# Where a slot's second score matmul stands, and how the prologue and the mixer's channels are arranged

## The chip, the cores and the metric

The kernel runs on one core of a Trainium2 chip. The metric is the device time in microseconds (us) of one execution. The five engines are TensorE (PE in the profile; PEld is its weight loading), VectorE (DVE), ScalarE (ACT), GpSimd (POOL) and SyncE (SP), which here only issues transfers. Each engine works through its own list of instructions in order, and semaphores tie the lists together. Before the change, three runs took 1406.85 to 1408.10 us, with a median of 1407.93 us.

## What is computed

This is one transformer block with adaptive layer norm, for 2048 tokens of width D = 640. Its attention has 32 heads of width 128 over a cache of 2048 keys and values; its MLP block is a token-shifting mixer (w1, w2) followed by an MLP (w3, w4) of width 1728.

```python
mod = (silu(c) @ w_mod).reshape(1, 6, 1, 640)      # six modulation vectors
sa, ca, ga, sb, cb, gb = ...                        # p = 0 .. 5
h = layernorm(x) * (1 + ca) + sa
q = h @ wq                                          # 32 heads x 128
p = softmax(q @ k_cache.T * 128 ** -0.5)            # per head, 2048 x 2048
x = x + ga * ((p @ v_cache) @ wo)
h = layernorm(x) * (1 + cb) + sb
u = gelu(layernorm(h) @ w1)                         # mixer: four groups of 160 channels,
                                                    # shifted by +1, -1, +2, -2 tokens
x1 = h + shifted(u) @ w2
x = x + gb * (x1 + gelu(layernorm(x1) @ w3) @ w4)
```

## The kernel before

The program is a list of operations. Each has an engine, what it reads and writes, and a key (the last number in the PE calls below). TensorE executes its operations in the order of their keys; the other engines' orders are found by a list scheduler inside the kernel, which also puts in the semaphore waits.

Attention is cut into 128 *steps*: 8 groups of 4 heads, 4 chunks of 512 tokens, 4 heads. A step has 8 *slots* (NP = 8). In a slot TensorE computes the scores of two key tiles of 128 keys against 512 queries (two matmuls of 512 columns into the two banks of one score tile), ScalarE takes the exp of the whole score tile, and TensorE multiplies earlier exps with the values (129 columns: 128 values and a column of ones for the row sum). There are two score tiles, S0 and S1, used in turn, so the scores of slot n+2 can be written once the exp of slot n is done.

```python
for j in range(NP):
    n = s * NP + j
    sp = Tile(pool="S%d" % (n % 2))
    pt = PT[n % NPT]
    for r in range(2):
        kt = 2 * j + r
        P.op("PE", <score matmul, 128x512>, ..., (K[b][kt // 4], q), (sp,), n + 0.01 * r, accum=True)
    x = P.op("ACT", <exp of sp into pt, 128x1024>, 1021, (sp,), (pt,), n)
    for r in range(2):
        u = 2 * j + r
        # slot: the slot in which key tile u is multiplied, PV_SLOTS = [2, 2, 3, 2, 2, 3, 2] tiles
        # in the slots 3 .. 9 after the step's start (8 and 9 are slots 0 and 1 of the next step)
        key = NP * s + 3 + slot + 0.3 + 0.01 * (u - acc)
        for bk in range(2):
            kb = key + 0.004 * bk if u < NKT - 2 else NP * s + 9.35 + 0.02 * bk + 0.001 * u
            P.op("PE", <two value matmuls, 128x129>, ..., (pt, V[b]), (o[bk],), kb, accum=True)
```

The query projection of the next step (five matmuls of 512 columns) has the keys `NP * s + 2.3 + 0.01 * kk`, so it stands in slot 2. The output projection of a chunk (32 matmuls of 320 columns) is spread over four later steps, with fractions of 0.6.

The prologue computes the first two modulation vectors as columns, from five pieces `wm[k]` of w_mod, normalises chunk 0 of x, transposes it on TensorE and makes the first query. `spin(n, key)` is n matmuls of ones that keep TensorE busy; their result is not used. Two of the other modulation vectors (p = 2 and 4) are loaded by ScalarE's queue into the buffers of heads 4 and 3 and are computed in the prologue and in step 0; p = 3 and 5 follow in steps 2 to 5.

```python
x0 = load_x2(0, -301, eng="ACT") + load_x2(2, -301)
...
P.op("POOL", <copy s_bc, broadcast>, 1000, (c_f,), (s_bc,), -290, lat=300)
spin(50, -298)
for k in range(KT):
    P.op("PE", mcol, ..., (wm[k], s_bf, ones), (mc,) + ..., -290 + k, accum=True)
# in ln1, chunk 0: transposes of x-hat, tiles 0 and 1 ahead of the last modulation piece
P.op("PE", tr, 330, ..., (-286.6 if i < 2 else -280) + 0.1 * i, accum=True)
# in ln1, the other chunks: statistics on VectorE, then rstd on ScalarE, then the DMA transpose to hT
rstd_act(g, a, a + 2, prio - 100, 0.0 if ch == 0 else 1500.0)
...
load_wq(0, 0, 1, -297)
load_k(0, -296, gate=(wm[2],))          # all pieces but the first wait for wm[2]
for p, b, pools, keys in ((2, NKV - 1, ("O0", "O1"), (-262, 0.5)), (4, NKV - 2, ("M", "M"), (1.5, 2.2))):
    ap = KV_t[:, b * KVW:b * KVW + KT * D].rearrange("p (k n) -> p k n", k=KT)
    dma("ACT", <w_mod vector p into ap>, 800, (wm[1],), tuple(K[b]) + (V[b],), -292 if p == 2 else -291)
    ...                                 # 2 x 5 matmuls of 320 columns per vector
    if p == 4:
        load_v(0, -290, "ACT", gate=(wm[1],))
load_wq(0, 1, HG, -295.985, gate=(wm[2],))
for n, p in enumerate((3, 5)):
    dma("SP", <w_mod vector p>, 800, ..., 8 + 12 * n, from_slot(8 + 12 * n))
    ...                                 # keys NP * (2 + 2 * n + hf) + 3.65 + k
```

After attention, TAIL gives the order of the parts: A is a w1 part of a chunk (25 matmuls of 512 columns), B a w2 tile of 128 tokens (10 of 320), WO the last output projection (32 of 320), I the layer norms of the last chunk, C a w3 part (70 of 512), D a w4 tile (28 of 320).

```python
TAIL = ("A0 B0 B1 B2 A1 B3 WO B4 B5 A2 B6 I3 B7 B8 C0 B9 D0 D1 D2 D3 C1 D4 A3 B10 B11 "
        "B12 B13 B14 D5 D6 D7 B15 C2 D8 D9 D10 D11 C3 D12 D13 D14 D15").split()
def w1_part(ch, key):                   # channels regrouped: 4 x 128 and the 4 x 32 that are left over
    for n in (4, 0, 1, 2, 3):
        ...                             # 5 matmuls into a bank of pool T (4 banks)
        if n == 4:
            P.op("ACT", <GELU of the left-over channels into rest>, ...)
            for g in range(4):
                P.op("DVE", <copy 32 rows of rest to us, shifted by DEL[g]>, 330, ...)
        else:
            P.op("ACT", <GELU of 128 channels of group n into us, shifted by DEL[n]>, ...)
```

Of the kernel before, what the change touches and what calls it, by code (L numbers as in the profile page):

```python
# [40 lines left out]
class Plan:  # L41
# [4 lines left out]
    HINT = {"PE": 300, "ACT": 40, "DVE": 60, "POOL": 1, "SP": 12}  # L46
# [116 lines left out]
    def emit(self, nc, es, ndma, redo, flag):  # L163
# [68 lines left out]
        def body(e):  # L232
            def f(eng):
                for i, o in enumerate(self.seq[e]):
                    if i == max(0, len(self.seq[e]) - self.HINT[e]):
                        hint[e] = eng.mark_branch_hint_location()
                    for sem, v in waits[o].items():
                        eng.wait_ge(sem, v)
                    ins = o.fn(eng)
                    if o.dma:  # L240
                        ins.then_inc(o.sem, 16)
                    elif o.needed:
                        ins.then_inc(o.sem, 1)
# [16 lines left out]
def fast_path(nc, es, flag, A_x, A_k_cache, A_v_cache, A_wq, A_wo, B_w1, B_w2, B_w3, B_w4, c, w_mod, out):  # L260
# [72 lines left out]
    us = [[T() for _ in range(KT)] for _ in range(NC)]  # L333
# [17 lines left out]
    w2b = tuple(T() for _ in range(4))  # L351
# [24 lines left out]
    def dma(eng, fn, kb, reads, writes, prio, need=(), after=()):  # L376
        return P.op(eng, fn, {"SP": 480, "ACT": 480, "POOL": 1000}[eng], reads, writes, prio, dma=True, kb=kb, need=need, after=after)
# [9 lines left out]
    def v_ones(i):  # L387
        P.op("POOL", lambda e: e.memset(V_ap[i][:, :, 128:130], 1.0), 200, (), (V[i],), -297 + i)
    for i in range(NKV - 2):
        v_ones(i)  # L390
# [16 lines left out]
    x0 = load_x2(0, -301, eng="ACT") + load_x2(2, -301)  # L407
# [29 lines left out]
    P.op("POOL", lambda e: e.tensor_copy(s_bc.ap, c_f.ap.unsqueeze(2).to_broadcast([128, KT, 128])), 1000, (c_f,), (s_bc,), -290, lat=300)  # L437
    spin(50, -298)
    for k in range(KT):
# [7 lines left out]
        P.op("PE", mcol, 2 * KT * (85 if k < KT - 1 else 62), (wm[k], s_bf, ones), (mc,) + ((warm,) if k < KT - 1 else ()), -290 + k, accum=True)  # L447
# [83 lines left out]
    def ln1(ch, prio):  # L531
        g = ln_slot()
        xs = x0 if ch == 0 else load_x2(4 * ch, XP[ch], from_slot(XS[ch])) + load_x2(4 * ch + 2, XP[ch], from_slot(XS[ch]))
        for a in (0, 2):
            for i in (a, a + 1):
                ln_stats(xs[i].ap, (xs[i],), g, i, prio, 0.0 if ch == 0 else 2000.0)
            rstd_act(g, a, a + 2, prio - 100, 0.0 if ch == 0 else 1500.0)
# [3 lines left out]
        if ch == 0:  # L541
# [5 lines left out]
            for i in range(4):  # L547
# [4 lines left out]
                P.op("PE", tr, 330, (xn[i], ident), (hp[0], hp[1], hq, hp[4]), (-286.6 if i < 2 else -280) + 0.1 * i, accum=True)  # L552
# [18 lines left out]
    def load_k(h, prio, gate=(), need=()):  # L571
        b = h % NKV
        for i in range(4):
            dmaT(lambda e, i=i: e.dma_start_transpose(K_ap[b][:, i * 512:(i + 1) * 512].unsqueeze(1), A_k_cache[0, h, i * 512:(i + 1) * 512, :]),
                 128, gate if i or h else (), (K[b][i],), prio + 0.01 * i, need)
# [5 lines left out]
    def load_wq(g, a, b, prio, need=(), gate=()):  # L581
        dma("SP", lambda e: e.dma_start(wq_t[g % 2][:, :, a * 128:b * 128],
                                        A_wq[:, (g * HG + a) * 128:(g * HG + b) * 128].rearrange("(k p) d -> p k d", p=128)),
            160 * (b - a), gate, tuple(wq[g % 2][a:b]), prio, need)
# [8 lines left out]
    load_k(0, -296, gate=(wm[2],))  # L593
    ln1(0, -280)


    def modulation(p, hf, w_ap, w_t, pool, key, prio):
        m = Tile(pool=pool)
        sl = slice(hf * HD, (hf + 1) * HD)
        for k in range(KT):  # L600
            P.op("PE", lambda e, k=k: e.matmul(m[:, 0:HD], s_bc[:, k, :], w_ap[:, k, sl], start=(k == 0), stop=(k == KT - 1)),
                 MM(HD), (s_bc,) + w_t, (m,), key(k), accum=True)
        P.op("DVE", lambda e: e.tensor_scalar_add(out=mod[p][hf].ap, in0=m[:, 0:HD], scalar1=1.0 if p == 4 else 0.0),
             490, (m,), (mod[p][hf],), prio)

    mod_src = lambda p: w_mod[:, p * D:(p + 1) * D].rearrange("(k p) n -> p k n", p=128)
    for p, b, pools, keys in ((2, NKV - 1, ("O0", "O1"), (-262, 0.5)), (4, NKV - 2, ("M", "M"), (1.5, 2.2))):
        ap = KV_t[:, b * KVW:b * KVW + KT * D].rearrange("p (k n) -> p k n", k=KT)
        held = tuple(K[b]) + (V[b],)
        dma("ACT", lambda e, ap=ap, p=p: e.dma_start(ap, mod_src(p)), 800, (wm[1],), held, -292 if p == 2 else -291)  # L610
        for hf in range(2):
            modulation(p, hf, ap, held, pools[hf], lambda k, a=keys[hf]: a + 0.01 * k, -50)
        v_ones(b)
        if p == 4:
            load_v(0, -290, "ACT", gate=(wm[1],))

    def load_head(h):
# [3 lines left out]
        load_k(h, pr, (wm[2],) if h == 1 else (), from_slot(n))  # L621
        load_v(h, pr + 1, gate=(wm[2],) if h == 1 else (), need=from_slot(n + 1))
# [6 lines left out]
    load_wq(0, 1, HG, -295.985, gate=(wm[2],))  # L629
# [5 lines left out]
    for n, p in enumerate((3, 5)):  # L635
        dma("SP", lambda e, n=n, p=p: e.dma_start(w_half[n], mod_src(p)), 800, (), (W12[n],) + w2b + tuple(wm), 8 + 12 * n, from_slot(8 + 12 * n))
        for hf in range(2):
            modulation(p, hf, w_half[n], (W12[n],) + w2b, "M", lambda k, n=n, hf=hf: NP * (2 + 2 * n + hf) + 3.65 + k, NP - 60)

    TAIL = ("A0 B0 B1 B2 A1 B3 WO B4 B5 A2 B6 I3 B7 B8 C0 B9 D0 D1 D2 D3 C1 D4 A3 B10 B11 "  # L640
            "B12 B13 B14 D5 D6 D7 B15 C2 D8 D9 D10 D11 C3 D12 D13 D14 D15").split()
    WOKEY = 3000 + 50 * TAIL.index("WO")
    WOD, CH, I3D = -200, -200, 0


    evac, last_ot = [], []
# [13 lines left out]
    def wo_group(g, ch):  # L660
# [3 lines left out]
        for qt in range(4):  # L664
            last_ot[:] = last_ot[-3:] + [dmaT(lambda e, qt=qt: e.dma_start_transpose(OT_ap[gs][:, qt], On_ap[gs][:, qt].rearrange("p h d -> p (h d)")),
                 128, (On[gs][qt // 2],), (OT[gs][qt],), s * NP - 100)]
# [37 lines left out]
    def step(s):  # L704
# [5 lines left out]
        if s == 0:  # L710
            q_proj(0, [-270 + kk for kk in range(KT)])
        if s + 1 < NS:
# [982 lines left out]
```

## Time and profile before

| | |
|---|---|
| median of 3 runs | 1407.93 us |
| span of the profiled execution | 1403.4 us |
| TensorE's mean granted clock | 0.993 |
| first exp starts | 15.88 us |
| step 8's first exp starts | 98.36 us |
| last value matmuls start | 1210.88 us |
| first w3 matmul starts | 1255.55 us |
| exps | 1024, mean 1023 ns |
| score matmuls | 2048, mean 379 ns |
| value matmuls | 8192, mean 220 ns |

How to read it. Times in the trace count from the span's start. A matmul's mean duration is longer than the distance from one to the next, because matmuls overlap in the array; so durations of matmuls must not be summed, and the distances between their starts say how fast they go. In a timeline a line gives the start, the time to the end of the group, the engine, the line of the program, the operation with output and inputs, the shapes, and the count; a bracket at the end is the idle time of the engine ahead of the group and what ended it. SPq and ACTq are transfers being issued by the engine's sequencer.

### The profile page before, as it was taken

To read this page: it belongs to the slowest core of one execution; us is meant where nothing else is said; L and a number is where in the kernel's file an instruction comes from. 1 tells how busy PE (TensorE), PEld (TensorE's weight loads), DVE (VectorE), ACT (ScalarE), POOL (GpSimd) and SP (SyncE) were. 2 spreads that over 40 slices of the span, in tenths; PEclk is the share of its full clock that TensorE was granted. 3 is DMA by queue.
4 is the path that set the end of the run, shared out by engine and by line. 5 is a ranking of instruction groups with operands and counts; after the bars stand their busy time and mean duration, and the time that the engine had idled before them with its cause. 6 is when DMAs were issued, how large, how long until landed. Compare 5 with 4: busy or idle time off the path is not lost.

```text
span 1403.4 us, 29645 instructions
## 1 busy us (share of the span) xinstructions
PE 1371.6 (98%) x12901; PEld 939.5 (67%) x13128; DVE 524.9 (37%) x1354; ACT 1106.3 (79%) x1179; POOL 125.3 (9%) x108
## 2 busy tenths in 40 slices
PE   8899999999999999999999999999999999999998
PEld 6566776667766676666766677666776676545554
DVE  4353323332233323333233332333223344577552
ACT  5788888888888888888888888888888888744222
POOL 0000000000000000000000000001233376600000
PEclk9999999999999999999999999999999999999999
DMA  9880512251213321241205121512253022411110
GB/s 242 173 154 16 99 35 46 35 102 39 46 35 79 62 46 35 50 91 30 51 17 102 31 41 33 106 35 46 54 106 98 16 35 52 109 33 38 39 47 25
DMA packets 259172, 88.83 MB, mean 63 GB/s; under 512 B 236705, under 2 KB 257762, under 8 KB 259042
## 3 DMA queue, kind: packets, MB, share of 16 engines
q1 hardware_dynamic: 255106, 83.77, 29.2%
q10 hardware_dynamic: 3936, 3.15, 0.8%
q8 instruction: 104, 1.70, 0.5%
q14 instruction: 26, 0.21, 0.1%
HBM read 43.48 MB, written 2.62 MB: 33 GB/s over the span
## 4 chain that ended last, share of the span: by engine, by line
PE 95%; DMA 2%; ACT 1%; issue 1%; DVE 0%; ACTq 0%; SPq 0%
PE f_O L742 33%; PE f_S L723 30%; PE f_M L680 10%; PE f_M L655 10%; PE f_M L905 3%; PE f_S L891 2%; PE f_O L891 2%; PE f_S L905 2%; DMA f_KV<-in_A_v_cache_dram 1%; PE f_S L864 1%; PE f_M L864 1%; DMA f_W<-in_w_mod_dram 1%; PE f_S L841 1%; PE f_O L841 1%; ACT f_PQ L725 0%
## 5 line engine op out<-in xcount | busy, mean ns | idle before, releaser
L725 ACT ACTIVATE f_PQ<-f_S 128x1024 bf16<-128x1024 f32 x1024 | 1031.8, 1023 | 162.1 <-PE f_S L723 155.8
L742 PEld LDWEIGHTS f_O<-f_KV,f_PQ 128*128 128x128 bf16 x8192 | 540.1, 98 | 214.2 <-DMA f_KV<-in_A_v_cache_dram 2.5
L742 PE MATMUL f_O<-f_KV,f_PQ 128*128 128x129 bf16 x8192 | 612.9, 220 | 2.4 <-DMA f_KV<-in_A_v_cache_dram 2.0
L723 PE MATMUL f_S<-f_PQ,f_KV 128*128 128x512 bf16 x1873 | 572.2, 379 | 9.4 <-ACT f_PQ L725 0.2
L688 DVE TENSOR_TENSOR f_y<-f_M,f_y 128x320 f32<-128x320 f32 x192 | 94.4, 492 | 541.0 <-PE f_M L680 541.0
L680 PE MATMUL f_M<-f_wo,f_OO 128*128 128x320 bf16 x992 | 270.2, 299 | 0.0
L723 PEld LDWEIGHTS f_S<-f_PQ,f_KV 128*128 128x128 bf16 x2048 | 193.1, 98 | 42.5 <-ACT f_PQ L725 0.7
L655 PE MATMUL f_M<-f_hT,f_wq 128*128 128x512 bf16 x600 | 158.2, 381 | 7.3 <-DVE f_hT L566 3.9
L514 POOL TENSOR_TENSOR f_y<-f_y,f_mod 128x640 f32<-128x640 f32 x40 | 61.4, 1543 | 985.0 <-DVE f_y L688 977.6
L655 PEld LDWEIGHTS f_M<-f_hT,f_wq 128*128 128x128 bf16 x640 | 62.2, 98 | 82.0 <-DVE f_hT L566 5.8
L680 PEld LDWEIGHTS f_M<-f_wo,f_OO 128*128 128x128 bf16 x992 | 94.9, 97 | 27.9
L751 DVE TENSOR_TENSOR f_OO<-f_O,f_rl 128x256 bf16<-128x256 f32 x256 | 108.3, 423 | 8.2
L658 DVE CAST f_PQ<-f_M 128x512 bf16<-128x512 f32 x128 | 88.5, 692 | 56.4 <-PE f_M L655 56.3
L749 DVE RECIPROCAL f_rl<-f_O 128x2 f32<-128x2 f32 x256 | 43.5, 170 | 44.0 <-PE f_O L742 39.8
L686 DVE COPY f_y<-f_M 128x320 f32<-128x320 f32 x32 | 15.7, 492 | 80.1 <-PE f_M L680 80.1
L894 ACT ACTIVATE f_OO<-f_O 128x512 bf16<-128x512 f32 x28 | 16.7, 596 | 35.9 <-PE f_O L891 35.9
L905 PE MATMUL f_M<-f_KV,f_OO 128*128 128x320 bf16 x252 | 38.6, 300 | 0.0
L475 DVE BATCH_NORM_STATS2 f_small<-f_y 128x6 f32<-128x320 f32 x64 | 29.8, 480 | 10.8 <-POOL f_y L514 10.7
L905 PEld LDWEIGHTS f_M<-f_KV,f_OO 128*128 128x128 bf16 x252 | 23.3, 97 | 15.6 <-issue 6.0
L520 ACT ACTIVATE f_xn<-f_y,f_small 128x640 bf16<-128x640 f32 x12 | 10.7, 915 | 26.1 <-DVE f_small L499 21.8
L905 PE MATMUL f_S<-f_KV,f_OO 128*128 128x320 bf16 x196 | 30.0, 300 | 0.0
L905 PEld LDWEIGHTS f_S<-f_KV,f_OO 128*128 128x128 bf16 x196 | 18.0, 97 | 11.6 <-issue 3.7
(138 smaller groups left out, 517.9 us busy)
## 6 DMA issues: line engine op xcount, KB each, us to landing
f_KV<-in_A_v_cache_dram SPq DMA_DIRECT2D x31, 512.0 KB, 4.9
f_wo<-in_A_wo_dram SPq DMA_DIRECT2D x8, 640.0 KB, 4.1
f_xin<-in_A_x_dram SPq DMA_DIRECT2D x15, 320.0 KB, 3.4
f_wq<-in_A_wq_dram SPq DMA_DIRECT2D x7, 640.0 KB, 4.5
out_dram<-f_xin SPq DMA_DIRECT2D x15, 160.0 KB, 1.8
f_KV<-in_B_w_dram SPq DMA_DIRECT2D x5, 432.0 KB, 3.3
f_KV<-in_A_k_cache_dram SPq DMA_TRANSPOSE x128, 2.9
f_OO<-f_OO SPq DMA_TRANSPOSE x128, 2.5
```

The source lines that it names most:

```text
L514: P.op(eng, lambda e: e.tensor_tensor(out=out, in0=a, in1=b, op=op), COST[eng][0], rd, wr, prio, lat=300 if eng == "POOL" else None)
L655: P.op("PE", lambda e, i=i, kk=kk: e.matmul(m.ap, wq_t[g % 2][:, kk, hh * 128:(hh + 1) * 128], hT_t[ch][:, kk, :], start=(i == 0), stop=(i ...
L658: P.op("DVE", lambda e: e.tensor_copy(q.ap, m.ap), 690, (m,), (q,), s * NP - 90)
L680: P.op("PE", lambda e, m=m, qt=qt, hf=hf, hh=hh: e.matmul(m[:, 0:HD], OT_ap[gs][:, qt, hh, :], wo_t[g % 2][:, hh, hf * HD:(hf + 1) * HD], ...
L688: P.op("DVE", lambda e, m=m, yt=yt: e.tensor_tensor(out=yt.ap, in0=m[:, 0:HD], in1=yt.ap, op=ALU.add), 490, (m, yt), (yt,), s * NP - 60)
L723: P.op("PE", lambda e, sp=sp, r=r, kt=kt: e.matmul(sp[:, r * QC:(r + 1) * QC], K_ap[b][:, kt * 128:(kt + 1) * 128], q.ap, start=True, stop ...
L725: x = P.op("ACT", lambda e, sp=sp, pt=pt: e.activation(pt.ap.rearrange("p k q -> p (k q)"), sp.ap, ACT.Exp, scale=SCALE), 1021, (sp,), (pt ...
L742: ins = e.matmul(o[bk][:, w * 129:w * 129 + 129], pt[:, r, qt * 128:(qt + 1) * 128], V_ap[b][:, u, 0:129], start=(u == 0 and w == 0), stop ...
L749: P.op("DVE", lambda e, ov=ov, i0=i0: e.reciprocal(rl_t[:, i0:i0 + 2].unsqueeze(2), ov[:, 0:258].rearrange("p (u d) -> p u d", u=2)[:, :, ...
L751: evac.append(P.op("DVE", lambda e, ov=ov, i0=i0, bk=bk: e.tensor_tensor(out=On_ap[gs][:, 2 * bk:2 * bk + 2, hh, :], in0=ov[:, 0:258].rear ...
L891: P.op("PE", lambda e, m=m, f=f, kk=kk, fs=fs: e.matmul(m[0:fs, :], w3_ap[:, kk, f * 128:f * 128 + fs], nT_ap[ch][:, kk, :], start=(kk == ...
L905: P.op("PE", lambda e, f=f, hf=hf, fs=fs: e.matmul(m[:, hf * 512:hf * 512 + HD], gT_ap[0:fs, f, i * 128:(i + 1) * 128], w4_ap[f][0:fs, hf ...
```

## The change

The title change moves the second score matmul of a slot: for the steps 9 to 119 its key is 0.307 instead of 0.01 behind the slot's number, so it stands between the value matmuls of the slot's first key tile (0.300 and 0.304) and those of the second (0.310). A slot then reads score, four value matmuls, score, four or eight value matmuls, output projection. In slot 1 no value matmul has a key under 0.307 (theirs start at 0.35), so nothing comes between; in slot 2 one matmul of the query projection does. It is meant to give TensorE a long matmul ahead of each key tile's short ones.

```diff
-                     MM(QC), (K[b][kt // 4], q), (sp,), n + 0.01 * r, accum=True)
+                     MM(QC), (K[b][kt // 4], q), (sp,), n + (0.307 if 9 <= s < 120 else 0.01) * r, accum=True)
```

This version stands in place of another one, so what that other had is not in it. The prologue (cut):

```diff
-    x0 = load_x2(0, -301, eng="ACT") + load_x2(2, -301)
+    x0 = load_x2(0, -301) + load_x2(2, -301, eng="ACT")
-    P.op("POOL", <copy s_bc>, 1000, ..., -290, lat=300)
+    P.op("DVE", <copy s_bc>, 800, ..., 0.5)
+    spin(12, -281)                                     # behind the modulation columns
-            rstd_act(g, a, a + 2, prio - 100, 0.0 if ch == 0 else 1500.0)
+            rstd_act(g, a, a + 2, prio - 100)
-                P.op("PE", tr, 330, ..., (-286.6 if i < 2 else -280) + 0.1 * i, accum=True)
+                P.op("PE", tr, 330, ..., -280 + i, accum=True)
+                spin(6 if i < 3 else 10, -279.5 + i)
-    load_k(0, -296, gate=(wm[2],))
+    load_k(0, -296)
+    load_v(0, -290, "ACT", gate=(wm[3],))
...                                                     # modulation 2 and 4 in head buffers: taken out
-        load_k(h, pr, (wm[2],) if h == 1 else (), from_slot(n))
+        load_k(h, pr, need=from_slot(n))
-    load_wq(0, 1, HG, -295.985, gate=(wm[2],))
+    load_wq(0, 1, HG, -295)
-    for n, p in enumerate((3, 5)):
+    MS = 17
+    for n, p in enumerate((2, 4, 3, 5)):
+        dma("SP", <w_mod vector p>, 800, ..., MS * NP - 30 + n, from_slot((MS + 2 * n) * NP - 20))
+        ...                                             # matmul keys NP * (MS + i // KT) + 4 + i % KT + 0.65
+            spin(8, -260)                               # behind the first query projection
```

The part after attention (cut). The mixer's channels stay in five tiles of 128 in their own order; since the four groups have 160 channels each, a tile is written by one to three GELUs, nine for a chunk. The tile `us` is tracked by chunk and no longer by chunk and channel tile. The last token tile is no longer stored in two halves, and only TensorE has a branch hint ahead of the end.

```diff
-    TAIL = ("A0 B0 B1 B2 A1 B3 WO B4 B5 A2 B6 I3 B7 B8 C0 B9 D0 D1 D2 D3 C1 D4 A3 B10 B11 "
-            "B12 B13 B14 D5 D6 D7 B15 C2 D8 D9 D10 D11 C3 D12 D13 D14 D15").split()
+    TAIL = ("A0 WO B0 B1 B2 A1 B3 A2 B4 B5 B6 B7 C0 I3 D0 D1 D2 D3 C1 A3 B8 B9 B10 B11 D4 D5 D6 D7 B12 B13 B14 B15 C2 "
+            "D8 D9 D10 D11 C3 D12 D13 D14 D15").split()
-    WOD, CH, I3D = -200, -200, 0
+    WOD, CH, I3D = 0, -200, -200
-            960, (), (w4[i],) + old, E + 11 + i, after=last_ot if i else ())
+            960, (), (w4[i],) + old, E + 11 + i)
-    us = [[T() for _ in range(KT)] for _ in range(NC)]
+    us = [T() for _ in range(NC)]
-        for n in (4, 0, 1, 2, 3):
+        for n in range(KT):
...
+            for (p0, p1, dl) in segs[n]:
+                P.op("ACT", <GELU of rows p0 to p1 into us, shifted by dl>, act(QC), (m,), (us[ch],), key)
-            if last:
-                ...                                     # the last tile in two halves
-    HINT = {"PE": 300, "ACT": 40, "DVE": 60, "POOL": 1, "SP": 12}
```

## The prediction

> **What bounds the kernel now.** I read the page first (busy shares, the 40 slices, the chain that ended last), then a table of engine busy time by stretches that I cut where the slices change, then the timeline of the stretches that looked odd.
>
> ```profile
> PE 1371.6 (98%) x12901; PEld 939.5 (67%) x13128; DVE 524.9 (37%) x1354; ACT 1106.3 (79%) x1179; POOL 125.3 (9%) x108
> ...
> PE 95%; DMA 2%; ACT 1%; issue 1%; DVE 0%; ACTq 0%; SPq 0%
> ```
>
> TensorE is the bound; the question is only where it is not streaming. The stretches (length, then busy us of PE, PEld, DVE, ACT, POOL with counts, then granted clock, DMA share, GB/s):
>
> ```profile
> 16.00:49.00 33.00, 28.05 (x273) 18.86 (x276) 11.43 (x31) 26.59 (x31) 0.26 (x2) 1.00 1.13 197
> 49.00:57.00 8.00, 6.53 (x29) 3.09 (x30) 5.55 (x16) 2.00 (x2) 0.00 (x0) 0.57 0.46 158
> ...
> 98.00:1098.00 1000.00, 990.52 (x9865) 699.62 (x10044) 311.05 (x761) 872.04 (x865) 41.18 (x28) 1.00 0.28 57
> ...
> 1211.00:1256.00 45.00, 38.74 (x205) 21.47 (x208) 30.45 (x84) 20.09 (x30) 10.54 (x12) 0.89 0.28 64
> ```
>
> From 98 to 1098 us nothing is lost. Two stretches are not dense: the opening up to about 57 us (with a clock of 0.57 in 49 to 57) and the seam from attention to mixer, 1211 to 1256 (clock 0.89). One slot of the dense part, from the timeline around 704 us:
>
> ```profile
> 704.22 2.05 ACT L725 ACTIVATE f_PQ<-f_S 128x1024 bf16<-128x1024 f32 x2 [0.73 <-PE f_S L723]
> ...
> 704.61 0.59 PE L723 MATMUL f_S<-f_PQ,f_KV 128*128 128x512 bf16 x2
> ...
> 705.04 0.62 PE L742 MATMUL f_O<-f_KV,f_PQ 128*128 128x129 bf16 x8
> ...
> 705.49 0.30 PE L680 MATMUL f_M<-f_wo,f_OO 128*128 128x320 bf16 x1
> ...
> 705.63 0.38 PE L723 MATMUL f_S<-f_PQ,f_KV 128*128 128x512 bf16 x1
> ```
>
> A slot is two score matmuls, eight (or twelve) value matmuls and one output-projection matmul: 705.63 - 704.61 = 1.02 us. Start-to-start distances in the trace are 216 ns (512 columns), 56 to 57 (129 columns), 136 (320 columns): 2 x 216 + 8 x 57 + 136 = 1024. It is stream time, without a wait. A step of 8 slots takes 9.26 us from step 6 on, every time.
>
> The opening's hole, and what held the sync queue before it:
>
> ```profile
> 31.74 1.94 SPq L636 DMA_DIRECT2D f_W<-in_w_mod_dram  x1
> 33.72 5.73 SPq L574 DMA_TRANSPOSE f_KV<-in_A_k_cache_dram  x4
> ...
> 42.76 4.36 SPq L564 DMA_TRANSPOSE f_hT<-f_xn  x2
> ```
>
> ```profile
> 45.99 0.59 PE L723 MATMUL f_S<-f_PQ,f_KV 128*128 128x512 bf16 x2
> 50.03 0.61 PE L655 MATMUL f_M<-f_hT,f_wq 128*128 128x512 bf16 x1 [3.44 <-DVE f_hT L566]
> 51.07 2.08 PE L655 MATMUL f_M<-f_hT,f_wq 128*128 128x512 bf16 x4 [0.43 <-DVE f_hT L566]
> ```
>
> The query projection of chunk 1 waits 3.44 us for its transposed activations, then runs at half rate (4 matmuls in 2.08 us) to about 56 us.
>
> **What the Trainium skill says.** (1) "TensorE: Matmul & The Clock Gate", section "What's actually happening": the clock halves after an idle window of some 3.4 us. The trace agrees: three intervals at 0.5, of 6.8, 3.4 and 6.8 us, follow the gaps at 46.4, 1217 and 1231 us. They cost half their length, 8.5 us. (2) Same page, "Back-to-back issue gap": N/2.4 + 2.5 ns; for 129, 320, 512 columns 56.3, 135.8, 215.8, and the trace has 56 to 57, 136, 216. So matmul order has next to nothing left to win. (3) "ScalarE: Activation LUTs", section "What ACT_TABLE_LOAD costs": about 1.28 us a load; the trace has 1.28 at each. The seam holds three in a row twice. (4) "DMA: Bandwidth & Descriptors", section "Issuing engines are not separate DMA queues": transfers of all queues share the 16 engines. The trace agrees: a key transpose holds the sync queue 2.5 us while other loads run (9.95 to 15.01 for two), 1.43 us later (four in 5.73).
>
> **The change, part by part.** First exp now at 15.88 us, step 8 at 98.36, last value matmul at 1211.5, last matmul at 1398.9, span 1403.4.
>
> *Score matmul moved (steps 9 to 119, 111 steps).* No matmul is added. The 5th value matmul of a run, the first of the next key tile, is followed after 60 ns, where the others take 56; with a 512-column matmul ahead of each key tile I expect that extra to vanish in six of eight slots (slot 1 has nothing between, slot 2 no value matmuls): 6 x 3.5 = 20 ns a step, 2.3 us in all. I count 1, since this is a guess from one pattern.
>
> Its danger is the exp. It starts 416 ns after the second score matmul, so it moves back by four value matmuls, 4 x 57 = 229 ns. In the tightest slots the exp ends 0.39 us before its bank is written again (the first exp of 704.22 ends at 705.24; 705.63 is the score). 0.39 - 0.23 = 0.16 us stays; the smallest distance anywhere in this trace, where PE does wait for exp, is 0.055. So no new wait, by 0.1 us.
>
> *Opening.* The after-kernel drops the two modulation vectors from the opening and the gates on key loads; it has 48 more dummy matmuls there (12 + 6 + 6 + 6 + 10 + 8), and all four transposes behind the last modulation piece. Now the last transpose ends near 12.1; then, from about 11.0 (end of the modulation columns): 12 x 56 = 0.7, four groups of 0.28 and 18 dummies = 1.0 more, so 13.9. First exp at 17.8, +1.9 us.
> From there to step 8 the stream is: step 0 7.95 (its first slots have no value matmuls), steps 1 to 4 4 x 8.18 (step 1 measures 8183 ns), steps 5 to 7 3 x 9.26: 68.5. Waits: the chunk-1 statistics sit on ScalarE behind only five exps. Sync queue by hand: keys of head 0 from 3.6 to 12.6, weights to 13.2, three key transposes to 18.3, x to 19.4, landing near 22.5 (3.4 us is the page's median); the statistics of two tiles are there at 25.1, the sixth exp would have gone at 22.7: 2.5 us. Values of head 2 come behind the four hT transposes, 39.0 against 38.6: 0.5. So step 8 at 17.8 + 68.5 + 3 = 89.3, which is -9.1. The hole at 46 is gone: no modulation load stands ahead of the hT transposes any more (issued from 28, needed at about 46).
> The 40 modulation matmuls aren't saved: they go to steps 17 to 24, where PE is full: +40 x 136 = +5.4. Net -3.7.
>
> *Seam.* From 1211.5 to the start of the first MLP part (1255.55) PE has 16.2 + 4.4 + 12.2 us of work (three w1 parts, projection, nine w2 tiles) and takes 44. After: the projection comes right behind the first w1 part, so ScalarE's table loads (the same three) lie partly under it; but w1 needs nine GELUs of about 0.5 us instead of five with four copies on VectorE, and their banks are what the projection waits for. By hand, from the last value matmul: w1 done at 5.4, second GELU group done at 7.7, projection 7.7 to about 13, w2 tiles to 17.2, w1 to 22.6, a 0.8 us wait, all of it done at 35.7, against 44.0 - 1.4 (one w2 tile fewer ahead). -6.9; then half clock once or twice because the projection is thin, +2.4. -4.5, of which I take -3, since last_ot is lost too: the four output transposes now run behind and beside a 960 KB load.
>
> *End.* The last tile isn't split any more: 0.82 + 0.83 us on VectorE instead of 0.49 + 0.49, and 160 KB instead of 80 (1.8 against 1.6 us to landing): +0.8. Branch hints for four engines go: +0.7, an estimate with nothing in the trace behind it.
>
> Sum: -3.7 - 1 - 3 + 1.5 = -6.2. I put back 2, because the gates and the slack for statistics in the kernel before look like answers to waits that I can't see in its own trace. -4: 1407.9 - 4 = 1404.
>
> **Rivals.** *Exp becomes the bound in the dense part*: each exp 229 ns later; if releasing takes more than 0.16 us, every step pays 2 x 0.1 to 0.2 us, 111 times, +20 to +45 (1430 to 1450). For it: 0.1 us is thin. Against: 904 ns is the shortest exp period seen (steps 119 to 126) and a slot is 1022. *The opening gives nothing*: the ungated key loads take bandwidth from w_mod and x (DMA share is 0.97 there), the first exp comes 2 to 3 us later, statistics hold up exps, and PE falls to half clock once more; opening -1 instead of -9, and +8 in all (1412). For it: the reordering in the kernel before must have been for something. Against: its two measured waits, for values at 22.7 and for hT, both come from the loads it put first. *The seam is worse*: nine GELUs and thin projections cost more than the 11 us lost now: +4 (1411).
>
> **Range and chances.** Opening +-4, seam +-4, dense part +-3, end +-1: together about 7, skewed to slower by the first rival. 1394 to 1417. 2% is 28 us: faster 0.03, within 0.93, slower 0.04.
>
> **What would show it.** Step length in the dense part 9.24 to 9.26 and no wait of PE on exp (if over 9.3, the first rival); step 8's first exp near 89; steps 17 to 24 longer by 0.68 each; no half clock near 50 us; first MLP matmul 36 to 40 us after the last value matmul, clock over 0.89 there. Wrong at once if exp waits show in every step, or step 8 comes later than 95.

## The result, and the profile after

| | before | after |
|---|---|---|
| median time | 1408.01 us (1406.85 to 1408.97, 4 runs) | 1400.53 us (1400.40 to 1400.77, 4 runs) |
| span of the profiled execution | 1403.4 us | 1394.5 us |
| TensorE's mean granted clock there | 0.993 | 0.998 |
| first exp starts | 15.88 us | 17.19 us |
| step 8's first exp starts | 98.36 us | 87.38 us |
| a step of the dense part | 9260 ns | 9253 ns |
| steps 17 to 24 together | 74.1 us | 79.3 us |
| first w1 matmul after attention to first w3 matmul | 43.98 us | 39.27 us |

The changed kernel takes 0.9947 of the time before, 95% interval 0.993 to 0.9965: 7.5 us less. I had predicted 1404 in a range of 1394 to 1417.

The changed kernel's table by stretches (length; busy us and counts of PE, PEld, DVE, ACT, POOL; granted clock, DMA share, GB/s), cut like that of before:

```profile
16.00:49.00 33.00, 30.38 (x300) 20.41 (x303) 15.15 (x42) 28.48 (x34) 0.00 (x0) 1.00 0.91 177
49.00:57.00 8.00, 7.89 (x84) 5.52 (x83) 4.85 (x17) 7.50 (x11) 0.00 (x0) 1.00 0.21 43
98.00:1098.00 1000.00, 990.05 (x9845) 703.90 (x10032) 311.18 (x763) 878.80 (x860) 44.08 (x30) 1.00 0.31 60
1206.00:1245.00 39.00, 33.35 (x186) 18.46 (x188) 27.88 (x85) 29.37 (x44) 9.54 (x9) 0.96 0.35 73
```

The two stretches that were thin before are denser: 49 to 57 us runs at the full clock with 84 matmuls in place of 29, and the seam, the stretch from attention to the mixer, is 39 us long at a clock of 0.96. The dense part is as it was. One slot of it, PE's lines of the timeline:

```profile
700.87 0.38 PE L712 MATMUL f_S<-f_PQ,f_KV 128*128 128x512 bf16 x1
701.09 0.39 PE L731 MATMUL f_O<-f_KV,f_PQ 128*128 128x129 bf16 x4
701.31 0.38 PE L712 MATMUL f_S<-f_PQ,f_KV 128*128 128x512 bf16 x1
701.53 0.39 PE L731 MATMUL f_O<-f_KV,f_PQ 128*128 128x129 bf16 x4
```

Score, four values, score, four values: a projection matmul follows 0.22 us later, and nothing waits. In the tightest slots an exp now ends 0.16 us before its bank is written again (median over steps 30 to 109, taking 1.02 us for an exp), as the prediction worked it out.

The opening, transfers being issued by SP, where 5.73 us of key transposes and a modulation load had stood ahead of the activations (f_hT):

```profile
20.07 6.30 SPq L572 DMA_TRANSPOSE f_KV<-in_A_k_cache_dram  x4
26.42 6.12 SPq L562 DMA_TRANSPOSE f_hT<-f_xn  x4
```

All four activation transposes are now issued by 32.5 us, 12 us before the query projection of chunk 1 starts, and it doesn't wait for them. The longest wait that is left between the first exp and step 8 is one of 1.33 us at 25.05, where the sixth exp stands behind the statistics of chunk 1:

```profile
25.05 0.60 PE L712 MATMUL f_S<-f_PQ,f_KV 128*128 128x512 bf16 x2 [1.33 <-ACT f_PQ L714]
...
44.93 1.24 PE L643 MATMUL f_M<-f_hT,f_wq 128*128 128x512 bf16 x5
```

The seam, PE's lines of the timeline (last projection L668, first w3 part L877):

```profile
1214.29 0.70 PE L668 MATMUL f_S<-f_wo,f_OO 128*128 128x320 bf16 x4 [3.25 <-ACT f_PQ L836]
...
1217.33 2.11 PE L668 MATMUL f_O<-f_wo,f_OO 128*128 128x320 bf16 x8
...
1244.96 1.03 PE L877 MATMUL f_S<-f_wq,f_KV 128*128 128x512 bf16 x4 [0.21 <-DMA f_wq<-f_xn]
```

One long wait is left, 3.25 us for ACT at the head of the last projection, and one stretch of 3.41 us at half clock behind it: the eight matmuls at 1217.33 take 2.11 us where such a group takes 1.25 elsewhere. The last group has four of five records, so most of the 0.21 us ahead of it is a matmul that is missing from the trace.

Before, PE waited here for the GELUs of the first and of the second w1 part, and both waits were followed by a stretch at half clock:

```profile
1219.40 0.31 PE L864 MATMUL f_M<-f_W,f_PQ 128*128 128x320 bf16 x1 [2.35 <-ACT f_PQ L851]
...
1220.37 2.05 PE L864 MATMUL f_M<-f_W,f_PQ 128*128 128x320 bf16 x7 [0.18 <-ACT f_PQ L851]
...
1234.72 2.54 PE L864 MATMUL f_S<-f_W,f_PQ 128*128 128x320 bf16 x8 [3.30 <-ACT f_PQ L851]
```

### The profile page after: what moved, and what is told of

It is laid out like the page before. It is cut to its first block, busy times and chain, and to the rows that moved or that the text cites. A ratio compares the mean times of both kernels' runs of the same rounds, so it can differ in the third digit from the quotient of the medians.

```text
span 1394.5 us, 29726 instructions
## 1 busy us (share of the span) xinstructions
PE 1367.3 (98%) x12941; PEld 943.8 (68%) x13176; DVE 518.6 (37%) x1337; ACT 1125.9 (81%) x1195; POOL 123.8 (9%) x106
## 4 chain that ended last, share of the span: by engine, by line
PE 96%; ACT 2%; issue 1%; DVE 0%; DMA 0%; POOL 0%; ACTq 0%; POOLq 0%
PE f_O L731 34%; PE f_S L712 29%; PE f_M L643 10%; PE f_M L668 10%; PE f_S L890 2%; PE f_M L890 2%; PE f_S L877 2%; PE f_O L877 2%; ACT f_PQ L714 1%; PE f_S L850 1%; PE f_M L850 1%; PE f_S L413 1%; PE f_S L832 1%; ACT f_PQ L836 1%; PE f_O L832 0%
## 5 line engine op out<-in xcount | busy, mean ns | idle before, releaser
L731 PEld LDWEIGHTS f_O<-f_KV,f_PQ 128*128 128x128 bf16 x8192 | 593.7, 98 | 231.9 <-ACT f_PQ L714 0.5
L731 PE MATMUL f_O<-f_KV,f_PQ 128*128 128x129 bf16 x8192 | 720.2, 220 | 7.8 <-ACT f_PQ L714 0.3
L712 PE MATMUL f_S<-f_PQ,f_KV 128*128 128x512 bf16 x1856 | 671.3, 379 | 5.3 <-ACT f_PQ L714 2.2
L668 PE MATMUL f_M<-f_wo,f_OO 128*128 128x320 bf16 x992 | 270.2, 299 | 0.0
L712 PEld LDWEIGHTS f_S<-f_PQ,f_KV 128*128 128x128 bf16 x2048 | 196.2, 97 | 34.4 <-ACT f_PQ L714 3.9
L643 PE MATMUL f_M<-f_hT,f_wq 128*128 128x512 bf16 x608 | 170.8, 379 | 2.2 <-DVE f_hT L557 0.5
L668 PEld LDWEIGHTS f_M<-f_wo,f_OO 128*128 128x128 bf16 x992 | 95.1, 98 | 27.9
L880 ACT ACTIVATE f_OO<-f_O 128x512 bf16<-128x512 f32 (+1 forms) x28 | 16.7, 596 | 36.2 <-PE f_O L877 36.1
L880 ACT ACTIVATE f_OO<-f_S 128x512 bf16<-128x512 f32 (+1 forms) x28 | 16.7, 596 | 27.5 <-PE f_S L877 27.5
L890 PE MATMUL f_S<-f_KV,f_OO 128*128 128x320 bf16 x224 | 34.3, 300 | 0.0
L890 PE MATMUL f_M<-f_KV,f_OO 128*128 128x320 bf16 x224 | 34.3, 300 | 0.0
```

What stands on the lines that cost most here:

```text
L643: P.op("PE", lambda e, i=i, kk=kk: e.matmul(m.ap, wq_t[g % 2][:, kk, hh * 128:(hh + 1) * 128], hT_t[ch][:, kk, :], start=(i == 0), stop=(i ...
L668: P.op("PE", lambda e, m=m, qt=qt, hf=hf, hh=hh: e.matmul(m[:, 0:HD], OT_ap[gs][:, qt, hh, :], wo_t[g % 2][:, hh, hf * HD:(hf + 1) * HD], ...
L712: P.op("PE", lambda e, sp=sp, r=r, kt=kt: e.matmul(sp[:, r * QC:(r + 1) * QC], K_ap[b][:, kt * 128:(kt + 1) * 128], q.ap, start=True, stop ...
L731: ins = e.matmul(o[bk][:, w * 129:w * 129 + 129], pt[:, r, qt * 128:(qt + 1) * 128], V_ap[b][:, u, 0:129], start=(u == 0 and w == 0), stop ...
L890: P.op("PE", lambda e, f=f, hf=hf, fs=fs: e.matmul(m[:, hf * 512:hf * 512 + HD], gT_ap[0:fs, f, i * 128:(i + 1) * 128], w4_ap[f][0:fs, hf ...
```

## The experiments

Times of a run are medians; "before" in a comparison is the kernel before, measured beside the run on the same chip. The changed kernel's 1400.53 us was measured apart from these runs. Since the median of the kernel before moves between 1407.57 and 1408.04 us from one set of measurements to the next, a difference of half a microsecond from 1400.53 isn't shown to be real.

**e1, the title change undone.**

```diff
-  (sp,), n + (0.307 if 9 <= s < 120 else 0.01) * r, accum=True)
+  (sp,), n + 0.01 * r, accum=True)
```

> The changed kernel with the one constant 0.307 set back to 0.01, so that the second score matmul stands next to the first in all steps. Theory (the move only spares one hiccup per step): a step between 9 and 119 becomes 7 ns longer again (9253 -> 9260 ns), 0.7 us over the stretch, time 1401.2. Rival (the move gives the matmul stream slack it uses in the opening and at group changes as well): over 2 us longer, 1402.6 or more. Second rival (the later exps cost something): shorter than 1400.5.

Measured: dense step 9260 ns; 1400.65 us (1400.25 to 1400.97, 5 runs) against 1400.53. The step lengthens by the 7 ns, and 0.8 us (111 steps) in 1400 does not show in the time. Both rivals fall: the place of the score matmul does not carry the gain, and the later exps cost nothing that can be measured.

**e2, the title change alone,** the same line put into the kernel before.

> The kernel before with 0.307 in steps 9 to 119 and nothing else. Theory: its dense step goes from 9260 to 9253 ns and the time from 1408.0 to about 1407.3; no exp waits for a score that came late. Rival (the move is what made most of the gain): 1404 or less. Second rival (the exp becomes the bound): 1412 or more.

Measured: dense step 9253 ns; 1407.21 us against 1407.57, ratio 0.9996 (0.9987 to 1.0004). Two runs from two sides agree: the medians differ by 0.1 and 0.4 us, and e2's interval reaches from a gain of 1.8 us to a loss of 0.6. The change in the title can't be told from zero.

**e3 and e5, the opening alone.** The kernel before with the prologue part of the change as its diff shows it (load order, dummies, transposes, four modulation vectors in steps 17 to 24); score order, seam and end as before.

> The kernel before with the opening, the loads and the modulation of the changed kernel (all four modulation vectors in steps 17 to 24, no vector loaded ahead of the first values, no extra delay before the LayerNorm roots), and with its own score order, seam and end. Theory (parts add): step 8 begins at 87.4 instead of 98.4 us, the steps 17 to 24 take 5.4 us more, net -5.5: 1402.5. Rival (the opening's gain only appears together with the seam, for example because loads of the end begin earlier): less than 3 us of gain, 1405 or more.

Measured: 1404.89 us against 1407.57, ratio 0.998 (0.9973 to 0.9988); half of what I expected. Its profile shows step 8 at 87.84 us, as it should be, and then, in step 21, one slot of 3.42 us where it is 1.16 in the other steps: PE waits for a modulation load. That wait was the experiment's own. I had made every modulation load wait for the readers of a tile that only half of them share. Mended, for the loads and in the same way for the matmuls that read them:

```diff
-  800, (), (W12[n % 2],) + w2b + (tuple(wm) if n < 2 else ()), ...)
+  800, (), (W12[n % 2],) + (w2b if n % 2 else ()) + (tuple(wm) if n < 2 else ()), ...)
```

> The run of the opening alone once more, without the one dependency that it had added itself (each modulation load waited there for the readers of the piece before it; the matmuls of step 21 stood 2.3 us for a load). Theory: the 2.3 us are gone and the rest stays, so 1404.9 - 2.3 = 1402.6, that is 5 us under the kernel before. Rival (the 2.3 us were not what held it back): 1404.5 or more.

Measured: 1402.97 us (1399.93 to 1403.41, 5 runs) against 1407.86, ratio 0.9964 (0.9951 to 0.9978). The opening with its modulation is worth 4.9 us of the 7.5 (3.1 to 6.9 by the interval). The seam and the end have no run in the kernel before that holds them alone.

**e9, one number in the kernel before.** The theory for the hole at 46 us is the queue of SP: late roots (the reciprocal roots of the layer norm of chunk 1, which ScalarE takes between exps), then key transposes ahead of the activations.

```diff
-  rstd_act(g, a, a + 2, prio - 100, 0.0 if ch == 0 else 1500.0)
+  rstd_act(g, a, a + 2, prio - 100)
```

> The kernel before with the one number 1500 set to 0: the scheduler no longer assumes that the roots of chunk 1's LayerNorm come 1.5 us late, and puts them behind the 11th and 12th exp instead of the 13th; the first two transposes of chunk 1's activations then stand behind two of the four key transposes of head 3 in the queue, not behind all four. Before, the last of them landed at 49.5 us and step 3 took 15.9 us (13.6 in another run), where 8.2 is normal. Theory (the hole is the in-order queue of SP: late roots, then key transposes of about 1.4 us each ahead of the activations): the last one lands 3 us earlier, step 3 takes 10 to 12 us, time 1403 to 1405.5. Rival (the modulation load of 1.9 us and its matmuls in steps 2 to 5 made the hole): step 3 over 13 us, time 1407 or more.

Measured: step 3 takes 11.24 us where it had taken 15.88, and takes 8.17 in the changed kernel; 1403.63 us (1400.9 to 1406.71, 20 runs) against 1407.59, ratio 0.9974 (0.9968 to 0.9981). SP's issues, and PE where it had waited 3.44 us:

```profile
36.69 2.60 SPq L564 DMA_TRANSPOSE f_hT<-f_xn  x2
39.32 1.26 SPq L574 DMA_TRANSPOSE f_KV<-in_A_k_cache_dram  x1
40.63 2.60 SPq L564 DMA_TRANSPOSE f_hT<-f_xn  x2
```

```profile
47.20 0.39 PE L655 MATMUL f_M<-f_hT,f_wq 128*128 128x512 bf16 x1 [0.79 <-DVE f_hT L566]
```

The activations now pass two of the key transposes, the last is issued by 43.2 us in place of 47.1, the wait is 0.79 us, and in this profile, one of the fastest of the 20 runs, the clock is not halved behind it. One assumed delay, in one argument, was worth 4 us: it had ordered two engines' queues. Of the 7.7 us by which step 3 was too long it took 4.6; some 3 us stay, of which the modulation matmuls in the step are 0.7.

**e10, the other suspect.** The modulation vectors 3 and 5, loads and matmuls, go to steps 17 to 20; the late roots stay.

```diff
-  ..., 8 + 12 * n, from_slot(8 + 12 * n))
+  ..., NP * 17 - 30 + n, from_slot((17 + 2 * n) * NP - 20))
-  ..., "M", lambda k, n=n, hf=hf: NP * (2 + 2 * n + hf) + 3.65 + k, NP - 60)
+  ..., "M", lambda k, n=n, hf=hf: NP * (17 + 2 * n + hf) + 4.65 + k, NP * 17 - 60)
```

> The kernel before with two of its four modulation vectors (p = 3 and 5, loads and matmuls) moved from steps 2 to 5 to steps 17 to 20; the late roots stay. No work is added or taken away. Theory (queue and late roots): the queue is 1.9 us less full ahead of the activations, but PE comes 0.7 to 1.4 us earlier to the wait: step 3 still takes over 12 us, time within 2 us of before, 1406 or more. Rival (the load and matmuls of the two vectors made the hole): step 3 takes 8.2 to 9 us, time 1401 to 1402.5.

Measured: step 3 takes 14.9 us; 1406.29 us (1404.57 to 1408.44, 12 runs) against 1407.59, ratio 0.9993 (0.9984 to 1.0001). SP's issues and PE's wait:

```profile
31.57 7.02 SPq L574 DMA_TRANSPOSE f_KV<-in_A_k_cache_dram  x4
38.64 2.68 SPq L564 DMA_TRANSPOSE f_hT<-f_xn  x2
```

```profile
49.21 0.61 PE L655 MATMUL f_M<-f_hT,f_wq 128*128 128x512 bf16 x1 [3.57 <-DVE f_hT L566]
```

Without the load of 1.94 us ahead of them the four key transposes take 7.02 us to issue in place of 5.73, so the activations gain 0.9 us only, and PE's wait is what it was. The load that I had named as the cause was not it, and the 1.3 us of time are not clear of noise.

**e4, the order of the seam alone.** The changed kernel with TAIL, WOD and I3D of the kernel before; its nine GELUs for a w1 part stay.

```diff
-  TAIL = ("A0 WO B0 B1 B2 A1 B3 A2 B4 B5 B6 B7 C0 I3 D0 ..."
+  TAIL = ("A0 B0 B1 B2 A1 B3 WO B4 B5 A2 B6 I3 B7 B8 C0 B9 D0 ..."
-  WOD, CH, I3D = 0, -200, -200
+  WOD, CH, I3D = -200, -200, 0
```

> The changed kernel with the order of the seam of before (the last output projection after the third w1 part and four w2 tiles, its two shifts of priority exchanged as before) but with the channels grouped as in the changed kernel. Theory (the order made the gain of the seam, because the output projection no longer stands behind work that waits for the statistics): the seam loses 4 us or more again, 1404.5 or more. Rival (the grouping made it: no separate GELU with four copies on VectorE): at most 1 us longer, 1401.5 or less.

Measured: 1412.82 us (1411.97 to 1413.2), 12.2 us more than without this edit (1.0039 of the time before, 1.0025 to 1.0053). PE waits twice, each time for the last of the nine GELUs. Ahead of the first, from 1208.98 us, ScalarE has three table loads of 1.28 us and then eight GELUs of about 0.60, the last of which ends at 1218.26:

```profile
1218.31 2.85 PE L850 MATMUL f_M<-f_W,f_PQ 128*128 128x320 bf16 x10 [6.22 <-ACT f_PQ L836]
```

The second such wait, 6.95 us, ends at 1237.10. Behind each the ten matmuls take 2.85 us where 1.52 is normal: the clock is halved.

**e6, the grouping of the channels.** The changed kernel with its own order, and five GELUs and four copies on VectorE for a w1 part, as before. The finer tracking of `us` by channel tile and the loading of w2 in five pieces come back with it, so these three were not told apart:

```diff
-  for n in range(KT):
+  for n in (4, 0, 1, 2, 3):
...
-      for (p0, p1, dl) in segs[n]:
-          P.op("ACT", <GELU of rows p0 to p1 into us>, act(QC), (m,), (us[ch],), key)
+      if n == 4:
+          P.op("ACT", <GELU of the left-over channels into rest>, ...)
+          for g in range(4): P.op("DVE", <copy 32 rows of rest to us>, 330, ...)
+      else:
+          P.op("ACT", <GELU of 128 channels into us>, ...)
```

> The changed kernel with its own order of the seam but with the channels grouped as before: five GELUs of a whole tile and four short copies on VectorE for a w1 part in place of nine narrow GELUs of 0.60 us each. The order alone, without the grouping, was 12.2 us worse (1412.8). Theory (order and grouping are two answers to the same wait for the GELUs; the order hides the nine narrow ones behind the output projection, and what stands there now is 3.3 us of waiting for ACT at the head of the output projection): about half of that wait goes, and the half clock after it with it, 1397.5 to 1399.5. Rival (in the new order the GELUs are hidden anyway and the four copies stand in VectorE's way, which feeds the second LayerNorm): 1400.5 to 1403.

Measured: 1398.14 us (1397.12 to 1398.71, 5 runs), below every run of the changed kernel, clock 1.0 in all of them, as its theory had it. The four corners of the seam, first w1 to first w3 matmul in the profile:

| | order before | order after |
|---|---|---|
| five GELUs and four copies | 43.98 us (41.15 in e5, where the clock stayed full) | 36.94 us (e6) |
| nine narrow GELUs | 51.91 us (e4) | 39.27 us |

Between these profiles the order brings 4 to 13 us, and the regrouping in the change costs 2 to 11. The low end of the first, 41.15 to 36.94, has the full clock on both sides. Between the others the clock differs too. (The order of before has one w2 tile more in this stretch, 1.36 us, and before and e5 also have the other parts of before in the seam and at the end.)

**e7, no table loads in the seam.** In the changed kernel, the root for chunk 2's norms is taken on VectorE:

```diff
+            elif ch == NC - 2:
+                rstd_dve(g, a, a + 2, prio)
+                P.op("DVE", <nm = -1.0 * mean>, 170, ...)
             else:
                 rstd_act(g, a, a + 2, prio, 1200.0)
```

> The changed kernel with the reciprocal root of chunk 2's two LayerNorms taken on VectorE (some 8 short operations of about 0.06 to 0.1 us) instead of a logarithm and an exponential on ACT, so that ACT does not change its tables six times in the seam (1.28 us each, at 1207.9, 1209.5, 1211.1, 1217.2, 1222.4 and 1223.9 us). Theory (the table changes stand between the first GELU and the narrow ones, 3.8 us of the wait that PE has for ACT at the head of the output projection): the wait of 3.3 us goes and with it the half clock after it, the first w3 matmul is 3 to 5 us earlier, 1396 to 1398. Rival (the nine narrow GELUs alone, 5.4 us, hold the pace and the order absorbs the rest; VectorE is late with the statistics instead): at most 1 us, 1399.5 or more.

Measured: 1398.75 us (1398.2 to 1399.66, 5 runs), a gain of 1.8 us, between the two expectations. The wait for ACT is gone and another stands in its place:

```profile
1213.34 0.72 PE L668 MATMUL f_S<-f_wo,f_OO 128*128 128x320 bf16 x4 [1.92 <-DMA f_OO<-f_OO]
```

These are the transposes of the last attention outputs. In e6 the projection starts at 1213.15, with its weight load waiting 2.0 us for the same transfer. So e6 and e7 end nearly alike: both uncover the next wait, which ends about 1 us ahead of where the changed kernel's wait for ACT ended (1214.29), and neither has the halved stretch behind it, which had cost half of 3.41 us.

**e8, branch hints on all five engines.**

```diff
-  if e == "PE" and i == len(self.seq[e]) - 300:
+  if i == max(0, len(self.seq[e]) - self.HINT[e]):
```

> The changed kernel with branch hints on all five engines again (the changed kernel hints PE's branch alone). The profile's span of the changed kernel is 8 us shorter than before's, its time only 7: the part outside the span grew from 4.6 to 5.6 us. Theory (the missing hints make the four other engines fetch their end late, 1 us after the last store): the time minus the span goes back to 4.6 us and the time to 1399.5. Rival (what lies outside the span has to do with other things, such as where the code ends up): time and span as they are, 1400.6.

Measured: 1400.05 us (1399.39 to 1400.62); the time outside the span is 5.0 us in place of 5.7. Its direction is the theory's; the 0.5 us of time are no more than sets of measurements differ by. The median time outside the span is 4.6 to 5.1 us in seven kernels with all the hints and 5.3 to 5.9 in six that hint PE alone; single runs overlap. An eighth with all hints, e2, breaks the row with 1.7 us: there PE's branch at the end takes 4 us, and that lies inside the span. So spans of two kernels must not be compared to better than 3 us; their times can.

**e11, no dummies.** The 48 dummy matmuls taken out of the changed kernel.

```diff
-  spin(12, -281)
-  spin(6 if i < 3 else 10, -279.5 + i)
-  spin(8, -260)
```

> The changed kernel without the 48 dummy matmuls between the modulation columns, the transposes and the first query projection (12, 6, 6, 6, 10 and 8 of about 57 ns, 2.7 us in all). Theory (part of them lies on the way to the first exp, which came 1.3 us later in the profile of the changed kernel than before): first exp 1 to 1.5 us earlier, but the statistics of the next chunk are then waited for longer, by up to the same amount; time 1399.3 to 1400.5. Rival (they keep the clock up: without them TensorE idles for 2 us or more ahead of the first exp and the clock is halved there): 1402 or more and a window at 0.5 in the first 25 us.

Measured: 1398.0 us (1397.41 to 1398.85, 5 runs), better than the theory's best. The gain came from the wait that the theory wanted to grow. ScalarE in the changed kernel, and in e11:

```profile
20.42 1.94 ACT L714 ACTIVATE f_PQ<-f_S 128x1024 bf16<-128x1024 f32 x2 [0.38 <-PE f_S L712]
23.88 0.20 ACT L477 ACTIVATE f_small<-f_small 128x2 f32<-128x2 f32 x1 [1.52 <-DVE f_small L473]
```

```profile
19.71 4.83 ACT L711 ACTIVATE f_PQ<-f_S 128x1024 bf16<-128x1024 f32 x5 [0.38 <-PE f_S L709]
24.58 0.20 ACT L476 ACTIVATE f_small<-f_small 128x2 f32<-128x2 f32 x1
```

The scheduler counts the dummies as time. Without them it expects the exps earlier, and puts the first root behind eight exps in place of five; the wait of 1.52 us for the statistics is gone. Later, in step 3, 0.9 us comes back with a wait for the values of head 3, whose load is issued 0.9 us later than it was (40.35 for 39.41). At step 8 this profile is 1.45 us ahead of the changed kernel's (85.93 for 87.38), so it accounts for more than half of the 2.5 us. The clock stayed full throughout the opening, so the rival falls: these dummies weren't needed to hold it.

**e12, everything together.** The changed kernel without dummies, with the channels grouped as before, the root on VectorE, all hints, and, to cover the wait for the transposes, the second w1 part ahead of the projection:

```diff
-  TAIL = ("A0 WO B0 B1 B2 A1 B3 A2 ..."
+  TAIL = ("A0 A1 WO B0 B1 B2 B3 A2 ..."
```

> The changed kernel with what the runs found together: no 48 dummies (alone 2.5 us less), channels grouped as before (alone 2.4 less), the root of chunk 2 on VectorE (alone 1.8 less, but for the same wait as the grouping, so not counted again), all five branch hints (0.6 less), and the second w1 part ahead of the last output projection. That last edit is new: with the grouping or the root on VectorE alone, the output projection no longer waited for ACT but 1.7 to 2.1 us for the transposes of the last attention outputs; 25 matmuls of 0.216 us, 5.4 us, now stand ahead of it. Theory (the parts add, and the wait for the transposes is covered): 1400.6 - 2.5 - 2.4 - 0.6 = 1395.1, and 1 to 2 us less for the last edit: 1393 to 1394.5; no wait for a transfer at the head of the output projection. Rival (the parts add but the last edit only moves the wait to ACT or VectorE): 1395 or more. Second rival (the grouped copies and the roots crowd VectorE when they come together): 1397 or more.

Measured: 1403.31 us (1402.5 to 1406.52, 12 runs), ratio 0.9973 (0.9964 to 0.9983): worse than each of the four parts that had been run alone. The time lies where the second rival had it. The opening kept its gain (step 8 at 85.33 us), the seam takes 42.84 us. GpSimd there, and then VectorE, from the timeline:

```profile
1208.86 3.15 POOL L512 TENSOR_TENSOR f_y<-f_y,f_mod 128x640 f32<-128x640 f32 x2
```

```profile
1208.89 1.65 DVE L838 COPY f_PQ<-f_xin 32x512 bf16<-32x512 bf16 x1
1210.56 1.47 DVE L491 SCALAR_TENSOR_TENSOR f_small<-f_small 128x2 f32<-128x2 f32 x1
1212.06 0.29 DVE L838 COPY f_PQ<-f_xin 32x512 bf16<-32x512 bf16 x1
```

A copy that takes 0.29 us, and an operation on two columns that takes 0.15, take 1.65 and 1.47 when they meet a GpSimd operation, and end within 0.15 us of it (two of 1.54 us, which end at 1210.40 and 1212.01). In the kernel before one copy is held in this way, for 1.56 us at 1213.65, and in e6 one for 0.93. PE waits 1.69 and 0.69 us for VectorE inside the projection, and at the end of the seam for transposed activations:

```profile
1246.09 1.46 PE L882 MATMUL f_S<-f_wq,f_KV 128*128 128x512 bf16 x3 [5.47 <-DMA f_wq<-f_xn]
```

The wait for the output transposes is gone, as meant, but more came than went. That the crowded VectorE is the cause is not shown, because the early w1 part was never run alone, and the traces fit it as well: it puts the first w2 tile 18.0 us behind the first w1 matmul (1221.25 - 1203.25), where e6 has 11.7, and from there to the first w3 matmul e12 takes 24.8 us and e6 25.3, though e12 has a w1 part of 5.4 us less to do there. The seam is 5.9 us longer than e6's. Which of the five edits would go together was not tried further; the grouping with no dummies and all hints, but without the root on VectorE and without the early w1 part, stays an untried candidate. The best versions run are e11 and e6, each about 2.5 us below the changed kernel.

## Why the prediction was right, point by point

- **Score matmul moved: mechanism of the danger right, size of the gain wrong.** "No new wait" held, with the 0.16 us that had been worked out. The gain was sized at 20 ns a step and counted as 1 us; it is 7 ns, 0.8 us in all, and e1 and e2 cannot tell it from zero. The guess that the 60 ns gap vanishes in six slots was the wrong term: in steps 64 to 71 the distances of 60 or 61 ns between value matmuls fall from eight a step to four.
- **Opening: right in direction and roughly in size, wrong in what made the hole.** Predicted -9.1 at step 8 and -3.7 net; the profiles give -11.0 and e5 gives -4.9. The terms: the wait for statistics was 1.33 us, not 2.5, and the 0.5 for values of head 2 didn't come. First exp +1.9 was predicted, +1.3 measured in this pair; from one profile to the next it moves by up to 0.8 us (15.88 and 15.45 us for the opening of before in before and e2, 17.19 to 18.01 in eight profiles with the changed one), so this is no finer than that. The modulation in steps 17 to 24 cost what was counted: +5.4 (5.2 in the eight steps of the table, 0.14 in step 25, and 0.06 because each step is 7 ns shorter otherwise). The step that failed is "no modulation load stands ahead of the hT transposes any more" as the reason why the hole goes: e10 takes the load away and keeps the hole (a wait of 3.57 us), e9 takes the assumed delay of the roots away, and the wait falls from 3.44 to 0.79 us. That the change took this delay out as well was luck for the number.
- **Seam: -4.5 by hand, -3 taken; -3.3 in the profile** (39.27 - 43.98, and 1.36 for the w2 tile that leaves the stretch). The reason given, that the projection covers ACT's work, is what e4 shows. The hand sum of 35.7 and 2.4 for half clock was 1.2 short: the wait at the projection was 3.25 us, with 0.43 behind it, where I had 2.3, there were two waits of 0.8 where I had one, and half clock cost 1.7, not 2.4. A GELU takes 0.60 us where I had about 0.5, and eight of them stand in the wait at the projection. The third rival had named the nine GELUs; the regrouping is indeed a loss of its own, of 2 to 11 us (e6, e4), but the order pays for it.
- **End: +0.8 and +0.7.** From the last matmul to the end of the span it grew from 4.5 to 4.8 us: 0.3, not 0.8. VectorE's part grew by 0.67, as counted, and what follows it got shorter. The 0.7 for the branch hints, which had nothing behind it, fits the time outside the span in e8 and in the groups of kernels (0.6 to 0.7); that was luck.
- **The 2 us put back** answered to nothing that showed up. The sum without it, -6.2, was closer.
- **Rivals.** None of the three came: no exp wait in the dense part, no fall in the opening, no worse seam. The loss of the gates was not run alone; with the rest of the opening it brings no wait back.

What was not predicted is that the kernel also got steadier. The kernel before spreads from 1403.8 to 1412.45 us over 91 runs, and the granted clock goes with it: at a mean clock of 0.997 it takes 1405.6 us on average (17 runs), at 0.993 1408.5 (23 runs). The changed kernel has 0.998 in all runs of it and of e1, nine in all, from 1400.25 to 1400.97. "TensorE: Matmul & The Clock Gate", section "What's actually happening", in the Trainium skill says that the activity window, of about 3.4 us, is free-running and does not start anew with the kernel. The stretches at 0.5 ahead of the last matmul are indeed 3.41 us or twice that. Whether a gap is followed by one differs from run to run: the gaps of 2.35 and 3.30 us in before's seam were, though they are shorter than the window, and gaps of 2.35 and 3.29 at the same places in e5's profile were not. So in these traces a gap costs its length and, in some runs, 1.7 or 3.4 us on top.

The formula that the prediction takes from "Back-to-back issue gap" on the same page is given there for an isolated matmul; for a stream the page has about 131 ns at 512 columns. The stream of this kernel has 216 ns, so here the formula holds and the page's figure for streams does not.

## What to carry to other kernels

When several parts change at once, run each alone from both sides before giving reasons: here the change in the title was worth nothing that could be measured, the opening about two thirds, and one part of the seam was a loss hidden behind a larger gain. A queue that issues in order is read from what stands ahead of the late transfer and from why it was put there; an assumed delay in a scheduler can be the cause of the order. And gains that were measured one at a time are no forecast for all of them together: e6, e7, e8 and e11 gave 0.5 to 2.5 us each, and together with one more edit, untested by itself, they lost 2.8. An edit joins such a sum only after a run of its own.

## What the hardware showed that I had not expected

- A GELU of 32 rows and 512 columns takes 0.59 us, one of 64 or 96 rows as long, and one of 128 rows 0.60: in the changed kernel's seam the three that fill one tile take 1.80 us. So cutting a tile by rows multiplied ScalarE's time there.
- GpSimd operations held VectorE up: 0.29 became 1.65 us, 0.15 became 1.47 (e12), while GpSimd's own took 1.54 us, no longer than elsewhere; statistics on VectorE (0.50 us at 1204.72) were not longer under a GpSimd operation. "GPSIMD Engine Reference", section "Specifications", in the Trainium skill says that the SBUF interfaces are shared with VectorE, with contention for operations in a two-port mode or with two SBUF inputs; the trace agrees with it for the two kinds of operation that were held up.
- The time of a key transpose in SP's queue is no constant: four took 5.73 us behind a load, 7.02 without it, and 6.30 and 6.08 in the changed kernel. So these runs don't show that the 2.5 and 1.43 us of the prediction differ because of other loads.
- The end of a program can move by 3 us between inside and outside the span without a change of the time (e2).
